# Reordering the tile loop of a routed expert layer on one core

## The chip, the core and the metric

The kernel runs on one core of a Trainium2 chip. The metric is the device time of one execution in microseconds (us). Engines are named as the profile names them: PE is TensorE (matmuls; PEld is its weight load), DVE is VectorE, ACT is ScalarE, POOL is GpSimd, SP is SyncE, which here only issues DMAs. Each engine works through its own queue in the order in which the kernel text issues its instructions.

## The reference

A long convolution by FFT, then two mixture-of-experts layers over the same 22784 tokens of width 128. Only the last layer is touched:

```python
logits = x @ w_gate + modality_bias[modality_id]
e_idx = np.argmax(logits, axis=1)
gate_w = softmax(logits)[arange(N), e_idx]
for e in range(E):                      # 8 experts, F = 1024
    mask = e_idx == e
    h = np.maximum(x[mask] @ w1[e], 0.0)
    out[mask] = gate_w[mask, None] * (h @ w2[e])
```

The token rows x of this layer are themselves a product: 32 softmax weights c per token times 32 slot outputs. The kernel folds those slot outputs into the first expert matrix, so a token's record is only its 32 weights, times its gate weight.

## The kernel before, in words

The first half of the span (convolution, first layer) is left as it is. Around 515 us the routing begins, and from about 538 us on the routed experts run in `routed_experts` (line 1175).

**Routing (class Routing, line 809).** Tokens are held as 178 groups of 128. The routing goes in parts (`CP`, line 39: groups 0 to 26, 26 to 64, 64 to 128, 128 to 178) and each part has chunks (`GB`, line 37). For a part: `choose` (argmax and softmax pieces), `offsets` (where each token's record goes; two matmuls, `pre`), and per chunk `prepare` (gate weight, position, masks); `table` (line 1032) makes the list that tells each tile of 256 tokens its place and its expert. These are some hundred small DVE instructions. `late_steps` (line 1155) hands them out one by one, each with a planned cost in us, and `spend(us)` (line 1371) issues as many as a credit allows; `need` (line 1376) issues all of them that a tile can't go on without, at once.

**Batches.** Two groups make a batch; there are 89. `prep(n)` (line 995) makes n batches (1 or 2): on DVE the product `m` (line 1006), on ACT its rounding into `hl` (line 1008, called the rounding here), on DVE the one-hot `oh` (line 1009) and two address columns (line 1011); its return value `rest` is the DVE subtraction (line 1015). `sort` (line 1019) then takes a batch: two matmuls (`srt`, line 1027), an ACT copy `so` (line 1029) and an indirect DMA on POOL that scatters the records to HBM (line 1144).

**Tiles.** There are 89 tiles. For tile k:

- `load_rec(k)` (line 1228): SP loads the records, two DMAs (lines 1234, 1235), after the scatters of all chunks up to the tile's own; `load_w(k)` (line 1242): SP loads the expert's weights into one of three buffers, skipped where the buffer holds them already, and only when the tile that used the buffer is done.
- `tokT(k)` (line 1249): two transposes on PE into `pst`, the addresses `ids` on DVE, and the cast `x` on ACT (line 1258).
- `l1(k, h)` for two halves (line 1260): 4 matmuls into `ph` (line 1267), ReLU on ACT into `hh` (line 1269), remainder on DVE into `hl` (line 1270).
- `l2(k, f)` for f = 0 to 7 (line 1272): 3 matmuls each into `acc` (lines 1280 to 1282).
- `out1(k)`: ACT copies `acc` to `yT` (line 1286); `out2(k)`: two transposes on PE into `pso`, ACT copy `y` (line 1293); `store`: two indirect DMAs on POOL (line 1305).

In PSUM, `pst`, `pso` and the table's `pr` share one buffer (tag t), `srt` and `pre` share another (tag s), and `ph` has two.

**The order in the loop (`run`, line 1310)** is written out by hand, and it is what sets the order on each engine. In loop step k it works on l2 of tile k, l1 of tile k+1, tokT of tile k+2, the records of tile k+3 and the output of tile k-1. On PE: l1(k+1) half 0, l2 f 0-1, pso(k-1), srt of the batch prepared in the step before, l2 f 2-3, l1(k+1) half 1, pst(k+2), l2 f 4-7. On ACT: yT, ReLU 0, y, so, rounding, ReLU 1, x. On DVE: remainder 0, routing, m and oh, remainder 1, ids, routing, subtraction, routing. `prep_to` (line 1198) says how many batches are prepared by step k: two per step up to step 6, then one per step, up to step 68. Ahead of the loop four batches are prepared and sorted, 5 us of routing (`PRE`) are issued, 16 matmuls on constants (`keep_warm`, line 1324) run on PE, and tile 0 and 1 are begun.

Of the kernel before, what the change touches and what calls it, by code (L numbers as in the profile page):

```python
# [15 lines left out]
I32 = mybir.dt.int32  # L16
# [7 lines left out]
NS, NE, F = 32, 8, 1024  # L24
# [4 lines left out]
NGR = NG // COLS  # L29
# [6 lines left out]
RW = 2 * NS + 2  # L36
GB = [0, 18, 22, 26, 34, 44, 54, 64, 80, 96, 112, 128, 144, 160, NG]
NC = len(GB) - 1
CP = (0, 3, 7, 11, NC)
PARTS = [(GB[a], GB[b], a, b) for a, b in zip(CP[:-1], CP[1:])]  # L40
PIECES = ((0, 7, 2), (7, 12, 3), (19, 16, 4), (35, 10, 3))
RT = NT // TM + 1
SPARE = NE * RT
PRE = 5.0
PACE = 0.25
GAP = 0.6
W1 = 4
W2 = 3
# [3 lines left out]
W6 = 3  # L52
W7 = 10
W8 = 4
W10 = 16
YBUF = 16
FAR = 1 << 20

# [750 lines left out]
class Routing:  # L809
# [185 lines left out]
    def prep(self, n):  # L995


        nc = self.nc
        i0 = self.prepped
        self.prepped += n  # L1000
        g0, n = COLS * i0, COLS * n
        g1 = g0 + n
        m = self.work("m", (4, BK, NS), 2)[:, :n]
        hl = self.rounded.tile([128, 4, BK, RW], F32R, name="hl4", tag="hl4", bufs=2)[:, :n]
        oh = self.rounded.tile([128, 4, LANES], F32R, name="oh", tag="oh", bufs=2)[:, :n]
        nc.vector.tensor_tensor(m, self.c[:, g0:g1].unsqueeze(2).to_broadcast([128, n, BK, NS]),  # L1006
                                self.gm[:, g0:g1].unsqueeze(3).to_broadcast([128, n, BK, NS]), op=ALU.mult)
        nc.scalar.copy(hl[:, :, :, :NS], m)
        nc.vector.tensor_tensor(oh, self.il.unsqueeze(1).to_broadcast([128, n, LANES]),
                                self.lane[:, g0:g1].unsqueeze(2).to_broadcast([128, n, LANES]), op=ALU.is_equal)  # L1010
        nc.vector.tensor_tensor(hl[:, :, :, 2 * NS:], self.eq[:, g0:g1].unsqueeze(3).to_broadcast([128, n, BK, 2]),
                                self.ab[:, g0:g1].unsqueeze(2).to_broadcast([128, n, BK, 2]), op=ALU.mult)

        def rest():
            nc.vector.tensor_tensor(hl[:, :, :, NS:2 * NS], m, hl[:, :, :, :NS].bitcast(F32), op=ALU.subtract)  # L1015
            self.batches += [(i0 + j, hl[:, COLS * j:COLS * j + COLS], oh[:, COLS * j:COLS * j + COLS]) for j in range(n // COLS)]
        return rest

    def sort(self, n, put):

# [154 lines left out]
def routed_experts(nc, tc, R, P, out, ro, tabs, put):  # L1175

    ident = P["ident"]
    with tc.tile_pool(name="p6", bufs=1, reuse_waits="tile") as sp, tc.tile_pool(name="p6p", bufs=1, space=PS, reuse_waits="tile") as pp:
# [8 lines left out]
        t, hid, x, acc, yT, ids = {0: new_rec()}, {0: new_hid()}, {0: new_x()}, {}, {}, {}  # L1187
# [6 lines left out]
        def due(k):  # L1194

            return GB[chunk_of(k) + 1] // COLS

        def prep_to(k):
            return min(NGR, max(due(k + 4), min(due(3) + 2 + 2 * k, 21 + k)))

        def prep(n):

            need(0, COLS * (ro.prepped + n))
            return ro.prep(n)

        def fill(e):

# [92 lines left out]
        def store(n, k1):  # L1300

            while n > 0 and outs and outs[0][0] <= k1:
                n -= 1
                k, j, d, y = outs.pop(0)
                i = nc.gpsimd.indirect_dma_start(out, bass.IndirectOffsetOnAxis(ap=d[:, j:j + 1], axis=0), y[:, j, :], None,  # L1305
                                                 bounds_check=NT - 1, oob_is_err=False)
                tc.declare_no_dep(i.ins, group="out", reason="every token is written once")
                tc.add_to_no_dep_group("out", i.ins)

        def run(k0, k1):  # L1310
            def go(f, k, *a):
                if k0 <= k < k1:
                    f(k, *a)
            go(load_rec, k0)
            go(load_w, k0, 2)
            while k0 == 0 and ro.prepped < due(3):
                prep(2)()
                ro.sort(2, put)
            for k in range(k0 + 1, k0 + 4):
                go(load_rec, k)  # L1320
                if k < k0 + 3:
                    go(load_w, k)
            spend(PRE)
            keep_warm(nc, pp, P["ones"], W10 if k0 == 0 else 0, tag="s", bufs=1)
            go(tokT, k0)
            for h in range(2):
                go(l1, k0, h)
            go(tokT, k0 + 1)
            for k in range(k0, k1):
                if 52 <= k < 52 + NE:  # L1330
                    fill(k - 52)
                go(out1, k - 1)
                if k > k0:
                    go(load_w, k + 2)
                    if not ro.batches:
                        go(load_rec, k + 3)
                go(l1, k + 1, 0)
                new = prep_to(k) - ro.prepped if k0 == 0 else 0
                assert new <= 2
                go(l2, k, 0, 1)  # L1340
                go(out2, k - 1)
                late_rec = k > k0 and len(ro.batches) > 0
                ro.sort(min(1, len(ro.batches)), put)
                spend(PACE)
                go(l2, k, 2, 3)
                ro.sort(len(ro.batches), put)
                if late_rec:
                    go(load_rec, k + 3)
                rest = prep(new) if new > 0 else None
                store(4, k - 2)  # L1350
                go(l1, k + 1, 1)
# [37 lines left out]
def build(nc, tc, I, O, dbg=None):  # L1389
# [13 lines left out]
    with tc.tile_pool(name="const", bufs=1) as cp:  # L1403
# [87 lines left out]
        close(prc)  # L1491
        close(plc)
        rqc, rq = pool("rq", side="right")
        tabs = [rq.tile([1, n, 3], I32, name=f"tab{i}") for i, n in enumerate((32, 32, 64))] + [rq.tile([1, 128 + 4, 3], I32, name="tab3")]
# [6 lines left out]
        with tc.manual_schedule():  # L1501
# [52 lines left out]
            ro.prep(1)()  # L1554
            run_all(seconds(0))
            ro.sort(1, put)
            ro.prep(2)()
            run_all(sums(0), seconds(1))
            push(1, 1)
            ro.sort(2, put)  # L1560
            adds.append(gate(3))
            for i in range(3):
                ro.prep(2)()
                if i == 1:
                    run_all(seconds(2, 3))
                ro.sort(2, put)
# [36 lines left out]
```

## Time and profile before

| what | us |
|---|---|
| median of 3 runs | 1064.74 (1056.84 to 1066.64) |
| the profiled execution | 1068.16 |
| its span, first to last instruction | 1066.3 |
| tiles 0 to 88, from the x of tile 0 to the last yT | 555.1 to 1056.0 |

Times below are from the start of the span. The tiles are told apart by the starts of their `yT` copies on ACT: tile k ends there.

### The profile page before, as it was taken

The numbers are of one execution on the slowest core, as the hardware profiler recorded it, in microseconds if no ns is written. First come the engines' busy times: TensorE is split into PE (matmuls) and PEld (weight loads), VectorE is DVE, ScalarE is ACT, GpSimd is POOL, SyncE is SP. The second block draws the span as 40 slices with busy tenths as digits, with TensorE's granted clock in tenths as the row PEclk, the third lists the DMA queues.
The fourth block names the chain that finished last, engine by engine and source line by source line (L and its number), as shares of the span: only waits on it lengthen the run. The fifth ranks groups of instructions, "written<-read, shape, count | busy, mean of one in ns | idle before, by whom it ended". The sixth has DMA issues, their size and how long they took to land.

```text
span 1066.3 us, 23059 instructions
## 1 busy us (share of the span) xinstructions
PE 929.7 (87%) x7758; PEld 834.5 (78%) x7758; DVE 709.8 (67%) x1445; ACT 594.8 (56%) x1141; POOL 515.2 (48%) x611
## 2 busy tenths in 40 slices
PE   6999999999997898999557777989888999898996
PEld 6888888888786897786246776888877888788996
DVE  1668677776775688953857767777776766564553
ACT  2565574755745556532324654666665666665673
POOL 2225737657388804531212644545554555555443
PEclk8999999999998999999668998999999999998998
DMA  9616748568478658999571221222222222222221
GB/s 279 173 38 178 243 147 252 164 200 244 132 242 290 239 141 309 360 406 340 157 237 27 61 53 46 64 56 64 64 59 56 64 69 77 61 64 56 61 63 40
DMA packets 135978, 156.66 MB, mean 147 GB/s; under 512 B 59823, under 2 KB 112975, under 8 KB 133436
## 3 DMA queue, kind: packets, MB, share of 16 engines
q1 hardware_dynamic: 125888, 137.43, 42.3%
q0 software_dynamic: 9968, 17.71, 5.1%
q8 instruction: 64, 1.05, 0.4%
q14 instruction: 58, 0.48, 0.1%
HBM read 227.39 MB, written 63.70 MB: 273 GB/s over the span
## 4 chain that ended last, share of the span: by engine, by line
PE 21%; DVE 9%; issue 8%; ACT 7%; POOL 2%; DMA 1%; another core or an unknown queue 1%; SPq 1%; POOLq 0%; ACTq 0%
PE ph L1267 6%; ACT hh L1269 6%; DVE hl L1270 5%; PE acc L1280 4%; PE acc L1281 4%; PE acc L1282 4%; PE srt L1027 2%; POOL out L1305 1%; PE pso L99 1%; DVE m L1006 1%; PE pst L99 1%; DVE hl L1015 1%; ACT x L1258 1%; DMA w<-s_w 1%
## 5 line engine op out<-in xcount | busy, mean ns | idle before, releaser
L1270 DVE SCALAR_TENSOR_TENSOR hl<-ph,hh 128x1024 fp32r<-128x1024 f32 x178 | 217.9, 1224 | 164.9 <-ACT hh L1269 116.9
L1305 POOL DMA_INDIRECT out<-y,ids x178 | 176.3, 990 | 89.5 <-issue 44.5
L1269 ACT ACTIVATE hh<-ph 128x1024 fp32r<-128x1024 f32 x178 | 182.1, 1024 | 63.4 <-PE ph L1267 38.2
L1280 PE MATMUL acc<-hh,w 128*128 128x256 f32 x712 | 211.6, 297 | 0.0
L1281 PE MATMUL acc<-hl,w 128*128 128x256 f32 x712 | 203.4, 286 | 0.0
L1282 PE MATMUL acc<-hh,w 128*128 128x256 f32 x712 | 203.3, 285 | 0.0
L1144 POOL DMA_INDIRECT s_rec<-so,dst x80 | 79.8, 997 | 179.7 <-ACT so L1029 158.1
L1267 PE MATMUL ph<-x,w 128*128 128x256 f32 x712 | 123.7, 297 | 45.8 <-ACT x L1258 30.7
L1267 PEld LDWEIGHTS ph<-x,w 128*128 128x128 f32 x712 | 99.2, 195 | 58.8 <-ACT x L1258 36.3
L1281 PEld LDWEIGHTS acc<-hl,w 128*128 128x128 f32 x712 | 138.0, 194 | 0.0
L1282 PEld LDWEIGHTS acc<-hh,w 128*128 128x128 f32 x712 | 138.0, 194 | 0.0
L1280 PEld LDWEIGHTS acc<-hh,w 128*128 128x128 f32 x712 | 137.4, 193 | 0.5 <-issue 0.4
L192 PEld LDWEIGHTS psx<-G,A 128*128 128x128 f32 x890 | 111.9, 196 | 19.8 <-DVE Y L203 13.2
L192 PE MATMUL psx<-G,A 128*128 128x128 f32 x890 | 124.5, 287 | 2.5 <-DVE A L137 1.3
L127 PE MATMUL psa<-fw,xs 128*128 128x180 f32 x640 | 109.8, 325 | 14.4 <-POOL xs L161 7.9
L127 PEld LDWEIGHTS psa<-fw,xs 128*128 128x128 f32 x640 | 99.6, 199 | 24.8 <-POOL xs L161 15.5
L137 DVE COPY A<-psa 64x360 f32<-64x360 f32 x160 | 88.4, 553 | 36.3 <-PE psa L127 32.0
L131 ACT COPY A<-psa 64x360 f32<-64x360 f32 x160 | 83.7, 523 | 41.1 <-PE psa L127 37.9
L216 ACT COPY yt<-psy 128x512 f32<-128x512 f32 (+1 forms) x92 | 52.7, 573 | 78.6 <-PE psy L99 54.0
L205 POOL TENSOR_TENSOR Y<-Y,V 128x256 f32<-128x256 f32 (+1 forms) x92 | 65.7, 714 | 62.9 <-DVE V L204 57.0
L203 DVE TENSOR_TENSOR Y<-psx,H 128x512 f32<-128x512 f32 (+1 forms) x92 | 61.9, 673 | 46.1 <-PE psx L192 45.4
L161 POOL COPY xs<-xr 89x512 f32<-89x512 f32 x68 | 45.7, 674 | 93.6 <-PE psa L127 73.7
(245 smaller groups left out, 1579.0 us busy)
## 6 DMA issues: line engine op xcount, KB each, us to landing
w<-s_w SPq DMA_DIRECT2D x88, 1536.0 KB
s_yt<-yt SPq DMA_DIRECT2D x88, 256.0 KB
xr<-x SPq DMA_DIRECT2D x16, 640.0 KB
xr<-s_yt SPq DMA_DIRECT2D x18, 512.0 KB
s_w<-ws SPq DMA_DIRECT2D x32, 256.0 KB
L<-s_yt SPq DMA_DIRECT2D x16, 512.0 KB
rt<-s_rec SPq DMA_DIRECT2D x89, 66.0 KB
rt<-s_rec SPq DMA_DIRECT2D x89, 64.0 KB
```

The lines of the kernel that those rows point to most:

```text
L127: nc.tensor.matmul(ps[:, i, :4 * NPAIR], x, fw1, start=True, stop=True)
L131: i = nc.scalar.copy(o, v)
L137: i = nc.vector.tensor_copy(o, v)
L192: nc.tensor.matmul(ps[:, m, :], A[:, 2 * i + m // 2, :, m % 2], G[:, 4 * i + m, :], start=True, stop=True)
L1144: d = nc.gpsimd.indirect_dma_start(rows, bass.IndirectOffsetOnAxis(ap=ro.dst[:LANES, i:i + 1], axis=0), o, None, bounds_check=SPARE * TB - ...
L1267: nc.tensor.matmul(ps[:, TM * j:TM * j + TM], w[k % 3][:, f:f + 128], x[k], start=True, stop=True)
L1269: nc.scalar.activation(o, ps, AF.Relu)
L1270: nc.vector.scalar_tensor_tensor(hl[:, 4 * h:4 * h + 4].rearrange("p j t -> p (j t)"), ps, 0.0, o.bitcast(F32), op0=ALU.max, op1=ALU.subtract)
L1280: nc.tensor.matmul(acc[k], wh, hh[:, f], start=(f == 0), stop=False)
L1281: nc.tensor.matmul(acc[k], wh, hl[:, f], start=False, stop=False)
L1282: nc.tensor.matmul(acc[k], wl, hh[:, f], start=False, stop=(f == 7))
L1305: i = nc.gpsimd.indirect_dma_start(out, bass.IndirectOffsetOnAxis(ap=d[:, j:j + 1], axis=0), y[:, j, :], None, bounds_check=NT - 1, oob_is ...
```

## The change

The loop's order is rewritten; no instruction of the tiles themselves changes. Per loop step k now:

- PE: l1(k+1) half 0, l2 f 0, pst(k+2), l2 f 1-2, pso(k-1), l2 f 3, l1(k+1) half 1, l2 f 4-5, srt, l2 f 6-7.
- ACT: yT, ReLU 0, x, y, ReLU 1, rounding, so.
- DVE: remainder 0, ids, subtraction of the batch prepared in the step before, m and oh of the new one, routing, remainder 1, routing twice.
- In steps 0 to 3 (`EARLY`) rounding, subtraction and sort of the two new batches stay in the same step, the rounding ahead of ReLU 1, the sorts ahead of l2 f 6-7.
- SP: weights of tile k+2 and records of tile k+3 at the head of each step. POOL: the two stores of tile k-2 split over the step, then the scatter.

Ahead of the loop, 7 routing steps come first, then two batches, tile 0's transposes and half 0, two more batches, tile 0's half 1, tile 1's transposes; the 16 constant matmuls are gone. Routing has five parts (0 to 26, 26 to 64, 64 to 96, 96 to 128, 128 to 178). The planned routing per step is 0.9 us, not 0.75. `pr` moves to the PSUM buffer of `srt`. Fewer batches are prepared in steps 4 to 18.

```diff
-CP = (0, 3, 7, 11, NC)
+CP = (0, 3, 7, 9, 11, NC)
-PACE = 0.25
+PACE = 0.9
+PACE2 = 0.9
+EARLY = 4
-W10 = 16
 def prep(self, n):
...
-        nc.scalar.copy(hl[:, :, :, :NS], m)
...
-        def rest():
+        def hi():
+            nc.scalar.copy(hl[:, :, :, :NS], m)
+
+        def lo():
             nc.vector.tensor_tensor(hl[:, :, :, NS:2 * NS], m, ...op=ALU.subtract)
...
-        return rest
+        return hi, lo
         def prep_to(k):
-            return min(NGR, max(due(k + 4), min(due(3) + 2 + 2 * k, 21 + k)))
+            smooth = due(3) + 2 + 2 * k if k < EARLY else k + 18 if k < 9 else min(27 + 13 * (k - 9) // 10, k + 21)
+            return min(NGR, max(due(k + 5) if k >= EARLY else 0, smooth))
 def run(k0, k1):
...
-            while k0 == 0 and ro.prepped < due(3):
-                prep(2)()
+            if k0 == 0:
+                run_late(7)
+                prep_all(2)
                 ro.sort(2, put)
-            for k in range(k0 + 1, k0 + 4):
+            for k in range(k0 + 1, k0 + 3):
                 go(load_rec, k)
-                if k < k0 + 3:
-                    go(load_w, k)
+                go(load_w, k)
+            go(tokT, k0)
+            go(l1, k0, 0)
+            if k0 == 0:
+                prep_all(2)
+                ro.sort(2, put)
+            go(l1, k0, 1)
+            go(load_rec, k0 + 3)
+            go(tokT, k0 + 1)
             spend(PRE)
-            keep_warm(nc, pp, P["ones"], W10 if k0 == 0 else 0, tag="s", bufs=1)
-            go(tokT, k0)
-            for h in range(2):
-                go(l1, k0, h)
-            go(tokT, k0 + 1)
+            new = None
             for k in range(k0, k1):
+                early = k0 == 0 and k < EARLY
+                old, new = new, None
...
                 if k > k0:
                     go(load_w, k + 2)
-                    if not ro.batches:
-                        go(load_rec, k + 3)
+                    go(load_rec, k + 3)
+                store(1, k - 2)
                 go(l1, k + 1, 0)
-                new = prep_to(k) - ro.prepped if k0 == 0 else 0
-                go(l2, k, 0, 1)
+                go(l2, k, 0)
+                go(tokT, k + 2)
+                go(l2, k, 1, 2)
+                if old:
+                    old[1]()
                 go(out2, k - 1)
-                late_rec = k > k0 and len(ro.batches) > 0
-                ro.sort(min(1, len(ro.batches)), put)
-                spend(PACE)
-                go(l2, k, 2, 3)
+                go(l2, k, 3)
+                n = prep_to(k) - ro.prepped if k0 == 0 else 0
+                if n > 0:
+                    new = prep(n)
+                    if early:
+                        new[0]()
+                spend(pace(k) / 3)
+                store(3 if k < k0 + 6 else 1, k - 2)
+                go(l1, k + 1, 1)
+                if new and not early:
+                    new[0]()
+                go(l2, k, 4, 5)
+                spend(pace(k) / 3)
+                if new and early:
+                    new[1]()
+                    new = None
                 ro.sort(len(ro.batches), put)
-                if late_rec:
-                    go(load_rec, k + 3)
-                rest = prep(new) if new > 0 else None
-                store(4, k - 2)
-                go(l1, k + 1, 1)
-                go(tokT, k + 2)
-                go(l2, k, 4, 5)
-                spend(PACE)
-                if rest:
-                    rest()
                 go(l2, k, 6, 7)
-                spend(PACE)
+                spend(pace(k) / 3)
...
-        ro.psum = lambda *a, **k: pp.tile(*a, tag="t", bufs=1, **k)
+        ro.psum = lambda *a, **k: pp.tile(*a, tag="s", bufs=1, **k)
```

`pace(k)` returns `PACE` or `PACE2`, both 0.9; `prep_all(n)` calls `prep(n)` and then both functions that it returns; `run_late(n)` issues n routing steps. In `build`, one more table (64 entries) is allotted for the fifth part, and `ro.prep(n)()` becomes `ro.prep_all(n)`.

## Rows read from the trace of the kernel before

**Rows 1.** Busy time by stretch: us, each engine's busy us (instructions), granted clock, DMA.

```profile
540.00:554.00 14.00, 8.91 (x37) 7.04 (x37) 7.27 (x22) 2.38 (x6) 3.74 (x4) 0.50 0.75 244
566.60:625.10 58.50, 45.99 (x322) 41.80 (x322) 40.99 (x108) 32.69 (x65) 29.39 (x29) 0.91 0.19 50
625.10:928.20 303.10, 263.45 (x2028) 245.51 (x2029) 214.57 (x520) 188.69 (x373) 156.98 (x160) 0.98 0.24 61
928.20:968.60 40.40, 37.88 (x306) 36.22 (x305) 27.26 (x54) 28.44 (x55) 23.11 (x23) 1.00 0.24 61
988.10:1052.90 64.80, 64.08 (x540) 63.58 (x539) 37.57 (x46) 44.01 (x74) 29.08 (x31) 1.00 0.24 59
```

**Rows 2.** Timeline of tiles 64 and 65: start us, us, engine, line, op [idle before].

```profile
944.18 1.03 ACT L1269 ACTIVATE hh<-ph 128x1024 fp32r<-128x1024 f32 x1 [0.62 <-ACT yT L1286]
...
945.24 1.22 DVE L1270 SCALAR_TENSOR_TENSOR hl<-ph,hh 128x1024 fp32r<-128x1024 f32 x1 [0.55 <-ACT hh L1269]
...
946.38 0.41 DVE L1006 TENSOR_TENSOR m<-c,gm 128x256 f32<-128x256 f32 x1
...
947.14 1.02 ACT L1269 ACTIVATE hh<-ph 128x1024 fp32r<-128x1024 f32 x1
...
948.06 0.36 ACT L1258 CAST x<-pst 128x256 fp32r<-128x256 f32 x1
...
948.48 0.74 PE L1267 MATMUL ph<-x,w 128*128 128x256 f32 x4 [0.34 <-ACT x L1258]
...
949.32 1.02 ACT L1269 ACTIVATE hh<-ph 128x1024 fp32r<-128x1024 f32 x1 [0.62 <-ACT yT L1286]
...
952.94 0.28 PE L1282 MATMUL acc<-hh,w 128*128 128x256 f32 x1
```

**Rows 3.** Timeline of tiles without a sort, 992 to 999 us.

```profile
992.12 0.66 PE L1267 MATMUL ph<-x,w 128*128 128x256 f32 x4
...
993.22 1.03 ACT L1269 ACTIVATE hh<-ph 128x1024 fp32r<-128x1024 f32 x1 [0.37 <-PE ph L1267]
...
996.36 0.66 PE L1267 MATMUL ph<-x,w 128*128 128x256 f32 x4
...
996.62 0.37 ACT L1286 COPY yT<-acc 128x256 f32<-128x256 f32 x1 [0.39 <-ACT x L1258]
...
996.86 0.28 PE L1280 MATMUL acc<-hh,w 128*128 128x256 f32 x1
...
997.06 1.03 ACT L1269 ACTIVATE hh<-ph 128x1024 fp32r<-128x1024 f32 x1
...
999.15 0.54 SPq L1235 DMA_DIRECT2D rt<-s_rec  x1
```

**Rows 4.** What PE waited for from 625 to 969 us: total, times, longest.

```profile
PE ph L1267 <- ACT x L1258: 19.8, 17, 6.3
...
PE pst L99 <- ACT y L1293: 3.5, 9, 0.7
```

**Rows 5.** Timeline of the start, 537 to 542 us; two batches prepared at a time.

```profile
537.65 0.69 DVE L1006 TENSOR_TENSOR m<-c,gm 128x512 f32<-128x512 f32 x1 [0.92 <-DMA s_rec<-A,dst]
...
539.03 0.69 DVE L1015 TENSOR_TENSOR hl<-m,hl 128x512 fp32r<-128x512 f32 x1 [0.22 <-ACT hl L1008]
...
539.77 0.71 PE L1027 MATMUL srt<-hl,oh 128*72 128x264 f32 x2 [1.37 <-DVE hl L1015]
...
541.07 0.71 PE L1027 MATMUL srt<-hl,oh 128*72 128x264 f32 x2 [0.58 <-ACT so L1029]
```

**Rows 6.** Timeline: single long waits at 654, 971 to 976 us.

```profile
653.89 1.22 PE L1267 MATMUL ph<-x,w 128*128 128x256 f32 x4 [6.30 <-ACT x L1258]
...
970.78 0.54 SPq L1235 DMA_DIRECT2D rt<-s_rec  x1
...
973.37 0.33 PE L99 MATMUL pst<-identr,rt 128*128 128x128 f32 x2 [2.14 <-DMA rt<-s_rec]
...
975.95 1.02 ACT L1269 ACTIVATE hh<-ph 128x1024 fp32r<-128x1024 f32 x1 [4.67 <-remote]
```

More of the change, by code (lines that the diff above doesn't have):

```diff
@@ L1012, in prep, with prep_all @@
                                 self.ab[:, g0:g1].unsqueeze(2).to_broadcast([128, n, BK, 2]), op=ALU.mult)
-        def rest():
+        def hi():
+            nc.scalar.copy(hl[:, :, :, :NS], m)
+        def lo():
             nc.vector.tensor_tensor(hl[:, :, :, NS:2 * NS], m, hl[:, :, :, :NS].bitcast(F32), op=ALU.subtract)
             self.batches += [(i0 + j, hl[:, COLS * j:COLS * j + COLS], oh[:, COLS * j:COLS * j + COLS]) for j in range(n // COLS)]
-        return rest
+        return hi, lo
+    def prep_all(self, n):
+        for f in self.prep(n):
+            f()
     def sort(self, n, put):
@@ L1204, in prep, with prep_all, run_late, pace @@
             return ro.prep(n)
+        def prep_all(n):
+            for f in prep(n):
+                f()
+        def run_late(n):
+            for _ in range(n):
+                next(late)
+        def pace(k):
+            return PACE if k < 10 else PACE2
         def fill(e):
@@ L1334, in run @@
                     go(load_w, k + 2)
-                    if not ro.batches:
-                        go(load_rec, k + 3)
+                    go(load_rec, k + 3)
+                store(1, k - 2)
                 go(l1, k + 1, 0)
-                new = prep_to(k) - ro.prepped if k0 == 0 else 0
-                assert new <= 2
-                go(l2, k, 0, 1)
-                go(out2, k - 1)
-                late_rec = k > k0 and len(ro.batches) > 0
-                ro.sort(min(1, len(ro.batches)), put)
-                spend(PACE)
-                go(l2, k, 2, 3)
-                ro.sort(len(ro.batches), put)
-                if late_rec:
-                    go(load_rec, k + 3)
-                rest = prep(new) if new > 0 else None
-                store(4, k - 2)
-                go(l1, k + 1, 1)
-                go(tokT, k + 2)
-                go(l2, k, 4, 5)
-                spend(PACE)
-                if rest:
-                    rest()
+                go(l2, k, 0)
[3 more added lines that the diff above has]
+                    old[1]()
+                go(out2, k - 1)
+                go(l2, k, 3)
+                n = prep_to(k) - ro.prepped if k0 == 0 else 0
+                assert n <= 2
+                if n > 0:
[12 more added lines that the diff above has]
+                    new = None
+                ro.sort(len(ro.batches), put)
                 go(l2, k, 6, 7)
-                spend(PACE)
+                spend(pace(k) / 3)
+            assert not new
             out1(k1 - 1)
@@ L1493, in build @@
         rqc, rq = pool("rq", side="right")
-        tabs = [rq.tile([1, n, 3], I32, name=f"tab{i}") for i, n in enumerate((32, 32, 64))] + [rq.tile([1, 128 + 4, 3], I32, name="tab3")]
+        tabs = [rq.tile([1, n, 3], I32, name=f"tab{i}") for i, n in enumerate((32, 32, 64, 64))] + [rq.tile([1, 128 + 4, 3], I32, name="tab4")]
         P["identr"] = rq.tile([128, 128], F32R, name="identr")
@@ L1553, in build @@
             run_all(offsets, ro.gates(*PARTS[0][:2]), ro.positions(*PARTS[0][:2]), ro.masks(*PARTS[0][:2]))
-            ro.prep(1)()
+            ro.prep_all(1)
             run_all(seconds(0))
             ro.sort(1, put)
-            ro.prep(2)()
+            ro.prep_all(2)
             run_all(sums(0), seconds(1))
@@ L1562, in build @@
             for i in range(3):
-                ro.prep(2)()
+                ro.prep_all(2)
                 if i == 1:
```

## The prediction

> **What bounds the kernel now.** I read the busy table by stretch first. Cut at the starts of the copies to yT, [rows 1] holds 8 tiles in its second stretch (tiles 1 to 8, 7.31 us each), 53 in the third (9 to 61, 5.72 each), 8 in the fourth (62 to 69, 5.05) and 15 in the last (73 to 87, 4.32). Only the last has no sorting. There PE is busy 64.08 of 64.80 us at full clock: PE is the bound. Before that it isn't: 263 of 303 us.
>
> Then the timeline, for what the sorting tiles wait on. Follow the ring in [rows 2]: ReLU 0 at 944.18, its remainder on DVE +1.06, m +1.14 (DVE works in order), then on ACT the rounding and ReLU 1, and x after them at 948.06, which is +1.68; PE may start the next l1 +0.42, and that gives the next ReLU 0 +0.84. Sum 5.14, the tile. PE needs less: from l1 at 948.48 to its last product at 952.94, plus one spacing of 0.12 (l1's four take 0.50, [rows 3]), is 4.58. The same tile without a sort is 996.36 - 992.12 = 4.24, so a batch's two sort matmuls cost PE 0.34. The view of waits agrees: l1 stood 17 times, 19.8 us, for x [rows 4]. Routing steps on DVE lengthen the ring, and where a batch can't go on without routing they come all at once: PE stood 6.30 us at 653.89 [rows 6].
>
> **The steady tile with one batch.** The new order takes the ring apart. x stands right behind ReLU 0; m comes a whole half ahead of remainder 1; rounding stands behind ReLU 1 and is used a tile later. What remains:
>
> - PE: 4.58, plus what the new order adds. pst and pso share one PSUM buffer, and pso(k-1) now comes soon after pst(k+2), so PE, in order, waits there for x to be read out, and all of l2 f 3 to 7 stands behind it. Count from l1's first matmul. ReLU 0 starts +0.70 (997.06 - 996.36 [rows 3]); x starts 0.92 later (948.06 - 947.14 [rows 2]); PE goes on 0.42 after that: 2.04. PE gets to pso at 0.50 for l1, 0.36 for f 0, about 0.2 for pst (two transposes, an estimate from the spacing), 0.72 for f 1-2: 1.78. Wait 0.26. Bounds: nothing, if ACT were earlier, to 0.68, if ReLU 0 starts +1.10 as at 993.22. I take 0.27. Tile 4.85.
> - DVE: 27.26 / 8 = 3.41 a tile with one batch and little routing [rows 1]. In the third stretch it is 214.57 / 53 = 4.05, so routing is 0.64 on the average tile; twice that still makes 4.7. Hidden, with little to spare.
> - ACT: 28.44 / 8 = 3.56. Hidden.
> - SP: records of tile k+3 are issued as late as before but needed earlier. Second record DMA 2.53 after yT (999.15 - 996.62 [rows 3]), usable 2.59 later (973.37 - 970.78 [rows 6]): 5.12 after yT. pst wants them one tile later, l1 + 0.86, that is 4.85 - 0.26 + 0.86 = 5.45 after yT. Hidden by 0.33 in a sorting tile; in the last tiles (4.51 a tile) by nothing, but a late pst only eats into the wait at pso.
> - POOL: 23.11 / 8 = 2.89 for two stores and a scatter. Hidden; but the scatter now stands behind the stores and late in the tile, which costs at chunk borders (below).
>
> At this place the Trainium skill has a word against the change. The row: with pst far from pso the shared buffer cost PE 3.5 us over 344 us [rows 4]. The page "Perfetto Trace Analysis" (Optimizing Tensor Performance, Matmuls) says that independent groups should go through different PSUM banks, so that one's copy-out lies beside the next one's matmuls; here the two are put next to each other on one. By the old row the cost would be under 0.1 us a tile and my forecast some 17 us lower; by the rule the copy-out shows, as counted above. I follow the count.
>
> **Tiles 9 to 69.** Before: 303.1 + 40.4 = 343.5 for 61 tiles. That is 61 x 5.14 = 313.5 for the ring and 30 above it: the burst at 653.89, the routing, and waits with no releaser such as the 4.67 "remote" at 975.95 [rows 6]. After: 61 x 4.85 = 296. The burst goes: in planned costs, part two is now 32 groups, some 6 us to its first masks, and from tile 4 to 12 eight us are spent, where before 64 groups wanted over 9 and 6.4 were spent. Add 4 for three tiles with two batches (a second sort waits for the first one's copy, 1.30 at half clock [rows 5]); add 4 for nine chunk borders, where the record load waits for a scatter that now comes late in the tile (about 0.45 each, an estimate: scatter out 0.8 later than the load's usual time, less 0.33); keep 12 of the waits without releaser, which no edit touches. 316. Gain 27.
>
> **Tiles 70 to 88.** No sort, so nothing to win, and the wait at pso comes in: 19 x 0.27 = 5 lost.
>
> **Tile 0 to 8.** 7 routing steps now stand ahead of the first batch on DVE: it moves from 537.65 to about 539.7. With 2.1 for preparing, two sorts at 1.30 and x's copy, tile 0's half 0 can start near 544 (an estimate), but DVE goes on to the second pair of batches only after remainder 0 (about 548), their sort stands on PE ahead of half 1, and 5 us of planned routing follow on DVE before tile 1's remainder 0 near 563. Then two more batches and their sort stand ahead of tile 0's f 6-7. I get 571 for its yT, against 566.6.
>
> In tiles 1 to 3 everything is one chain through DVE: l1 to ReLU 0 0.70, remainder +1.06, m +1.2, rounding and ReLU 1 +1.24, remainder 1 +1.06, routing and subtraction +1.5, sort +0.74 (539.77 - 539.03 [rows 5]), second sort +0.95 (of the 1.30), end of it and f 6-7 +1.04: 9.5. Three of them are 28.5, where the trace before has 23.2; with a forced table in tile 2 (nine steps, 0.5) 29. Tiles 4 to 8 have one batch: 5 x 4.85 = 24.3 where before 35.3, plus 3 for waits without releaser. Sum: +4.4 + 5.8 - 8 = +2: the early tiles lose what the next ones win. Removing the constant matmuls wins nothing: x of tile 0 stood behind them, but DVE sets the new start.
>
> **Sum.** +2 - 27 + 5 = -20 against the profiled execution: 1068.2 - 20 = 1048. That execution lies 3.4 us above the median; against the median 1064.7 the forecast is 1045.
>
> **Rivals.**
>
> 1. *Fewer waits without releaser.* If the 12 + 3 us kept above come from the tight ring and go with it, 1030. For: several coincide with PE standing for ACT. Against: they end with nothing that the profile names, and some lie in tiles without a sort. 0.15.
> 2. *Half clock in the early tiles.* In the start the granted clock is 0.50, that is 1.2 GHz [rows 1], though PE is busy 8.9 of 14 us, and in tiles 1 to 8 it is 0.91. The new early tiles leave PE idle nearly half of 9.5 us. At half clock the PE links of the chain (l1 0.5, two sorts 0.64, f 6-7 0.72, drain 0.3) double: 2.2 a tile, four tiles, 9 us: 1054 to 1055, within 1%. For: the constant matmuls that raised the clock are gone. Against: tiles 4 on are dense. 0.09. The page "TensorE: Matmul & The Clock Gate" (HAM oscillation — how this bites in real kernels) has this as its rule: bursts parted by waits fall back to half rate each time. By that rule the four tiles pay it; the trace before agrees in so far as l1 after the wait of 6.30 took 1.22, not 0.66 [rows 3, 6].
> 3. *Late records.* If record loads come 0.6 later under the earlier pst (scatters and stores in the same stretch of the tile), sorting tiles lose up to 0.6 - 0.33 beyond the wait at pso, the last ones 0.3 to 0.5: some 20 us, 1065, no change. For: 0.33 is little. Against: same queue, same place as before, and the one long wait for records was 2.14 in 89 tiles. 0.07.
> 4. *The routing doesn't spread.* The burst stays because credits run short: +8 and 2 more, 1055. Against: the count above. 0.04.
> 5. *Slower: the shared PSUM buffer.* If ReLU 0 starts +1.10 in the common tile, as at 993.22 [rows 3], the wait at pso is 0.68, not 0.27: +0.41 in 85 tiles, 35 us: 1080. It equals the kernel before from a wait of about 0.27 + 20 / 85 = 0.50. For: yT, ReLU 0 and x now stand in one row on ACT between acc's end and pso. Against: ReLU 0 at +0.70 in the undisturbed tile. 0.10.
>
> **How the numbers follow.** The forecast 0.55; its own range, from the spread of its estimates (early tiles 4, wait at pso 0.05 x 85), 1036 to 1054. Rivals 0.15, 0.09, 0.07, 0.04, 0.10. A measurement of this kernel tells about 1% from no change, that is 1054.1 and 1075.4. Faster: 0.55 + 0.15 = 0.70. Within: 0.09 + 0.07 + 0.04 = 0.20. Slower: 0.10. The range takes in rivals 1 to 4 (low end a little under the first) and leaves out the last: 1027 to 1066.
>
> **What would show it.** Right: in tiles 20 to 60 l1 no longer waits for x; pso waits for x about 0.27 in nearly every tile; tiles near 4.85 to 5.0; the last ones near 4.5, slower than 4.24; tiles 0 to 3 near 9.5 with the sort waiting for the subtraction on DVE; no burst near tile 12. Wrong: last tiles at 4.24 (buffer free in time), sorting tiles still over 5.1, pst waiting for records in most tiles, or an early stage that ends well before 625 us.

## The result, and the profile after

The changed kernel took 1074.36 us (median of 4 runs, 1071.71 to 1082.97) beside 1062.12 for the kernel before (4 runs, 1056.84 to 1066.64): a ratio of 1.0137 [1.0093, 1.0181], slower by 0.9 to 1.8%. The forecast was 1045. Later, on other chips, the same two kernels gave 1037.04 and 1041.78 (12 and 17 runs): 0.9950 [0.9934, 0.9967], faster by half a per cent, which is less than the 1% that the forecast took for no change. Both have to be explained.

Cut at the starts of the copies to `yT`, in us; e5 and e6 are the same two kernels again on one other chip, and e3 and e7 two variants (below). The last row counts TensorE's semaphore updates that came late (a semaphore update is the signal by which an engine tells the others that a result is ready); it is explained under the timeline.

| tiles | before | changed | e6: before | e5: changed | e3 | e7 |
|---|---|---|---|---|---|---|
| tile 0 ends at | 566.6 | 571.6 | 568.6 | 570.3 | 571.7 | 564.4 |
| 1 to 3 | 23.3 | 32.4 | 21.9 | 32.2 | 33.6 | 21.7 |
| 4 to 8 | 35.2 | 30.2 | 29.6 | 25.9 | 24.5 | 28.6 |
| 9 to 69 | 343.6 | 340.8 | 329.8 | 308.5 | 301.1 | 302.4 |
| 70 to 72 | 19.4 | 14.9 | 14.2 | 14.5 | 14.3 | 14.6 |
| 73 to 87 | 64.8 | 69.1 | 63.4 | 68.4 | 65.6 | 65.1 |
| after tile 87 | 13.4 | 13.3 | 13.4 | 13.3 | 13.3 | 13.4 |
| span | 1066.3 | 1072.4 | 1041.0 | 1033.1 | 1024.1 | 1010.1 |
| late updates, 9 to 69 | 107 of 370 | 160 of 374 | 0 of 370 | 0 of 374 | 2 of 374 | 2 of 374 |

The busy table by stretch of the changed kernel, for the stretches of [rows 1] and, first, for tiles 1 to 3 alone (us; busy us of PE, PEld, DVE, ACT, POOL; clock; DMA):

```profile
571.60:604.00 32.40, 21.33 (x126) 18.86 (x126) 16.63 (x52) 12.96 (x24) 9.05 (x10) 0.81 0.13 32
...
571.60:634.30 62.70, 47.59 (x326) 43.86 (x326) 36.49 (x100) 31.00 (x60) 23.14 (x24) 0.88 0.17 44
634.30:929.60 295.30, 254.67 (x2033) 239.64 (x2031) 221.86 (x553) 189.34 (x378) 166.30 (x162) 1.00 0.25 63
929.60:975.00 45.40, 39.01 (x314) 36.80 (x313) 25.82 (x49) 28.06 (x56) 27.71 (x27) 1.00 0.26 66
989.90:1059.10 69.20, 67.00 (x541) 63.81 (x540) 37.78 (x45) 45.70 (x75) 29.21 (x31) 1.00 0.23 56
```

From 634 to 930 us PE is busy 255 of 295 us at full clock. It still isn't the bound there, though the ring of [rows 2] is gone.

The timeline of the changed kernel (start, us, engine, line, operation [idle before, releaser]): the start, tile 1, a tile at 708 us, and two tiles without a sort.

```profile
539.22 0.69 DVE L1007 TENSOR_TENSOR m<-c,gm 128x512 f32<-128x512 f32 x1 [1.22 <-DMA s_rec<-A,dst]
...
577.07 1.22 DVE L1290 SCALAR_TENSOR_TENSOR hl<-ph,hh 128x1024 fp32r<-128x1024 f32 x1 [0.79 <-ACT hh L1289]
...
578.51 0.68 DVE L1018 TENSOR_TENSOR hl<-m,hl 128x512 fp32r<-128x512 f32 x1
...
579.34 0.44 PE L1034 MATMUL srt<-hl,oh 128*72 128x264 f32 x2 [3.35 <-DVE t_of L1095]
...
582.99 1.10 PE L1287 MATMUL ph<-x,w 128*128 128x256 f32 x4
...
708.08 0.64 PE L1287 MATMUL ph<-x,w 128*128 128x256 f32 x4
...
708.39 0.98 POOL L1325 DMA_INDIRECT out<-y,ids  x1 [0.30 <-issue]
...
709.27 0.41 PE L1034 MATMUL srt<-hl,oh 128*72 128x264 f32 x2
...
710.12 0.28 PE L1302 MATMUL acc<-hh,w 128*128 128x256 f32 x1
...
710.34 1.02 ACT L1289 ACTIVATE hh<-ph 128x1024 fp32r<-128x1024 f32 x1 [1.93 <-PE srt L1034]
...
1008.22 0.37 ACT L1306 COPY yT<-acc 128x256 f32<-128x256 f32 x1 [0.47 <-PE acc L1302]
...
1009.99 0.20 PEld L100 LDWEIGHTS pso<-ident,yT 128*128 128x128 f32 x2 [0.25 <-ACT x L1278]
...
1012.85 0.37 ACT L1306 COPY yT<-acc 128x256 f32<-128x256 f32 x1 [0.53 <-PE acc L1302]
```

Where the forecast held: the start (539.22 for the first m, 539.7 forecast; [rows 5] had 537.65), tile 0 (571.6; 571), the wait of pso for x in the tiles without a sort (4.57 in the common tile, 4.63 in the one shown, beside 4.24 in [rows 3]), no burst near tile 12, and in tile 1 a sort that stood 3.35 us for remainder, routing steps and subtraction on VectorE.

Where it failed is the tile at 708 us. The second half of l1 starts at 708.08 and its four matmuls follow within 0.4. ReLU 1 needs nothing else, yet starts only at 710.34, when TensorE has already finished the tile; the view names the sort, for which ReLU 1 doesn't wait. The trace also records the semaphore events, which the views don't list: the update of that l1 was due at 708.73 and arrived at 710.32, those of the sort and of acc at 710.41 and 710.49, all three almost together. Meanwhile a store ran on GpSimd. I call an update late if it arrives more than 0.2 us behind its usual delay (0.30 after the start of a group's last matmul, 0.24 for pst; 0.01 after an instruction's end on ScalarE and VectorE; an update without a record of its own is dated by the next record, so its time is an upper bound, and counts are good to a few). In tiles 9 to 69 the kernel before has 107 such of TensorE, the changed one 160.

The waits of the changed kernel in tiles 9 to 69 (engine, line, waited for: us in total, times, longest):

```profile
ACT hh L1289 <- issue: 18.6, 30, 4.2
ACT hh L1289 <- PE srt L1034: 17.8, 11, 2.0
ACT hh L1289 <- PE ph L1287: 12.5, 15, 1.3
...
ACT so L1036 <- PE acc L1302: 11.5, 24, 0.7
...
PE pso L100 <- ACT x L1278: 24.7, 47, 1.8
...
PE srt L1034 <- ACT so L1036: 4.4, 4, 1.6
```

ReLU "waits" 11 times for a sort and 30 times for nothing, and the copy `so` 24 times for acc: each a wait whose true releaser signalled late. Counted by the true releaser, ReLU stood 49.5 us behind late updates of l1 in these tiles, in 57 waits; in the kernel before 18.0 us, in 27. l1's wait for x of [rows 4] is gone.

### The profile page after: what moved, and what is told of

Read it like the earlier page. It is cut to its first block, busy times and chain, and to the rows that moved or that the text cites. A ratio compares the mean times of both kernels' runs of the same rounds, so it can differ in the third digit from the quotient of the medians.

```text
span 1072.4 us, 22977 instructions
## 1 busy us (share of the span) xinstructions
PE 924.5 (86%) x7732; PEld 830.5 (77%) x7732; DVE 715.5 (67%) x1481; ACT 596.0 (56%) x1141; POOL 520.7 (49%) x613
## 3 DMA queue, kind: packets, MB, share of 16 engines
q8 instruction: 64, 1.05, 0.4%
## 5 line engine op out<-in xcount | busy, mean ns | idle before, releaser
L1325 POOL DMA_INDIRECT out<-y,ids x178 | 184.5, 1036 | 98.0 <-issue 46.2
L1300 PE MATMUL acc<-hh,w 128*128 128x256 f32 x712 | 217.8, 306 | 0.0
L1302 PE MATMUL acc<-hh,w 128*128 128x256 f32 x712 | 203.7, 286 | 0.0
L1151 POOL DMA_INDIRECT s_rec<-so,dst x80 | 76.7, 959 | 171.2 <-ACT yT L1306 86.2
L1287 PE MATMUL ph<-x,w 128*128 128x256 f32 x712 | 118.4, 290 | 5.0 <-DMA w<-s_w 5.0
L128 PE MATMUL psa<-fw,xs 128*128 128x180 f32 x640 | 110.9, 327 | 13.4 <-POOL xs L162 7.1
```

What stands on the lines that cost most here:

```text
L128: nc.tensor.matmul(ps[:, i, :4 * NPAIR], x, fw1, start=True, stop=True)
L1151: d = nc.gpsimd.indirect_dma_start(rows, bass.IndirectOffsetOnAxis(ap=ro.dst[:LANES, i:i + 1], axis=0), o, None, bounds_check=SPARE * TB - ...
L1287: nc.tensor.matmul(ps[:, TM * j:TM * j + TM], w[k % 3][:, f:f + 128], x[k], start=True, stop=True)
L1300: nc.tensor.matmul(acc[k], wh, hh[:, f], start=(f == 0), stop=False)
L1302: nc.tensor.matmul(acc[k], wl, hh[:, f], start=False, stop=(f == 7))
```

## The experiments

**e1 to e4: without the stores, and two edits of the changed kernel.** The edit of e1 (changed kernel) and e2 (kernel before):

```diff
-            for j in range(2):
+            for j in range(0 if 10 <= k < 67 else 2):
                 outs.append((k, j, d, y))
```

> The changed kernel, with the output stores of tiles 10 to 66 left out (GpSimd issues no indirect store there; the scatters stay). Theory 1, held signals: in the trace of the changed kernel the semaphore updates of TensorE that fall due 1.0 to 1.8 us after the start of a store on GpSimd arrive only at about 1.85, with the first packets of that store; the new order puts the second half of l1 and the sort there, so that ReLU 1 starts 1.0 to 1.6 late in some 18 of 61 tiles and the copy to so 0.6 late in most. Without stores those waits go: tiles 9 to 69 fall from 340.8 to about 318, one-batch tiles from 5.10 to about 4.85, the whole to about 1050. Theory 2, the new order's own chain (ReLU 0, x, pso, y, ReLU 1, so, yT in one row on ScalarE) makes 5.1: GpSimd is not in it, tiles 9 to 69 stay at 336 to 341, the whole at 1068 to 1074.

> The kernel before, with the output stores of tiles 10 to 66 left out. Theory 1: there the held signals fall mostly on pso and the sort, whose copies are not in the ring ReLU 0, remainder 0, m, rounding, ReLU 1, x, l1 of 5.14; ReLU 1 is late in 5 cases only. So little is won: tiles 9 to 69 from 343.6 to about 335, the whole near 1054. If it wins as much as the changed kernel does (over 18 us), the stores cost both orders alike and do not explain why the change failed.

e3 and e4:

```diff
-            ps = pp.tile([128, 2, 128], F32, name="pst", tag="t", bufs=1)
+            ps = pp.tile([128, 2, 128], F32, name="pst", tag="s", bufs=1)
```
```diff
                 go(out2, k - 1)
-                go(l2, k, 3)
...
                 go(l1, k + 1, 1)
+                go(l2, k, 3)
```

> The changed kernel with pst in the PSUM buffer of the sort instead of the one it shares with pso; nothing else. The wait of pso for x (30.7 us in 55 waits in the changed kernel's trace) goes. In the tiles without a sort, where nothing else is late, a tile falls from 4.57 to 4.24: 16 tiles, 5 us. Theory 1 (held signals set the sorting tiles): there little more comes, the whole falls by 5 to 10 us. Theory 2 (the shared buffer is what the forecast underrated): sorting tiles fall by 0.25 to 0.3 too, the whole by about 20 us.

> The changed kernel with the second half of l1 one product group earlier (ahead of l2 f 3 instead of behind it), 0.36 us sooner on TensorE. Theory 1: the stores start when so has been scattered, so the stretch in which signals are held does not move, and half 1 now mostly signals before it: the 18 late ReLU 1 become fewer than 6, tiles 9 to 69 fall by 10 to 18 us. Theory 2 (the chain on ScalarE): ReLU 1 still waits for y and starts hardly earlier: 0 to 5 us.

All four ran on a chip where the kernel before took 1042.43 (22 runs). e1: 1036.65, 0.9931 [0.9905, 0.9957]. e2: 1040.58, 0.9986 [0.9966, 1.0007]. e3: 1025.55, 0.9825 [0.9792, 0.9858]. e4: 1037.78, 0.9952 [0.9933, 0.9971]. e1 falls even below theory 1's number (309.6 for tiles 9 to 69, where it said 318), but e4, with all stores, has 309.1 too: in none of the four traces do more than 5 of TensorE's updates come late in these tiles, with stores or without. So theory 1 was not tested here, and on this chip the stores cost neither order much. What was tested: the shared buffer (theory 2 of e3: the sorting tiles fall too, though the whole by 11.5 us beside e5 below, not 20), and in e4 the place of the second half of l1, which gains nothing beside e5's 1037.04 below. e3's one-batch tiles take 4.56, e1's and e4's 4.86.

**e5 to e7: the two kernels again, and a version with the old start.** e7 is e3 with the prologue and, for tiles 0 to 3, the tile body of the kernel before:

```diff
-            if k0 == 0:
-                run_late(7)
+            while k0 == 0 and ro.prepped < due(3):
                 prep_all(2)
                 ro.sort(2, put)
...
             for k in range(k0, k1):
...
+                if k0 == 0 and k < EARLY:
...
+                    continue
                 store(1, k - 2)
```

> The changed kernel itself, beside the kernel before. In the first pair of traces TensorE's semaphore updates came late after stores (31 of 88 for ph and 43 of 62 for the sort in tiles 9 to 69); in the traces of the four variants not one did, with or without stores, and there the kernel before took 1042 us and not 1062. Theory 1: the late updates belong to the chip or its moment, not to the order of the kernel. Then where they are absent the changed kernel has one-batch tiles of 4.86, about 312 us for tiles 9 to 69 and 1037 to 1040 us in all, 0.2 to 0.6% below the kernel before; and where they are present again it is 1070 to 1080 and 1% above. Theory 2: the changed order itself (pst beside pso) brings them about, and the variants were cured by their edits: then 1054 to 1058 us beside 1042, and late updates in the trace.

> The kernel before itself, for a trace from the same chip as the changed kernel's. Theory 1: no late updates of TensorE; the ring of 5.14 stays, since it doesn't hang on them; the burst of routing near tile 12 stays (two tiles of 11.2 and 7.6); tiles 9 to 69 take about 331 us instead of 343.6 and the tiles without a sort 4.24. Theory 2 (the late updates are part of this kernel): about 343 us for these tiles.

> The changed kernel with pst in the sort's PSUM buffer, and with the beginning of the kernel before: its prologue (all first batches sorted ahead of tile 0, constant matmuls, no early routing) and its tile body for tiles 0 to 3; the new order from tile 4 on. Theory 1 (in tiles 0 to 3 the new order puts preparing, sorting and remainders in one chain through VectorE inside the tile, 9.5 to 12 us a tile, where the old body spreads it over two tiles): tile 3's yT comes 15 to 16 us earlier than with the new start (at 589 instead of 605), tiles 4 to 8 stay near 25, and the whole falls by about 14, to 1010 to 1013 where the kernel before takes 1042. Theory 2 (the early tiles wait for the routing itself, whatever the order): what tiles 0 to 3 win comes back as waits in tiles 4 to 13, and the whole falls by less than 5.

On a third chip: e5 1037.04 beside 1041.78, 0.9950 [0.9934, 0.9967]; e6 1042.84 (one run); e7 1013.04, 0.9728 [0.9701, 0.9754]. Hardly any late updates in all three. Theory 1 held for all three: the late updates are not the order's own, and with the old start tile 3 ends at 586.1 instead of e3's 605.3, of which tiles 4 to 69 give back 5.5. The waits of e5 in tiles 9 to 69, and a tile of its timeline:

```profile
ACT y L1313 <- PE pso L100: 33.2, 61, 0.6
ACT hh L1289 <- PE ph L1287: 30.0, 61, 1.2
...
PE pso L100 <- ACT x L1278: 7.3, 42, 0.2
PE pst L100 <- DMA rt<-s_rec: 5.5, 9, 1.6
```
```profile
916.37 0.64 PE L1287 MATMUL ph<-x,w 128*128 128x256 f32 x4
...
917.11 1.03 ACT L1289 ACTIVATE hh<-ph 128x1024 fp32r<-128x1024 f32 x1
...
918.03 0.36 ACT L1278 CAST x<-pst 128x256 fp32r<-128x256 f32 x1
...
918.45 0.44 PE L100 MATMUL pso<-ident,yT 128*128 128x128 f32 x2 [0.17 <-ACT x L1278]
...
919.75 1.02 ACT L1289 ACTIVATE hh<-ph 128x1024 fp32r<-128x1024 f32 x1 [0.46 <-PE ph L1287]
...
921.22 0.64 PE L1287 MATMUL ph<-x,w 128*128 128x256 f32 x4
```

This is the tile as forecast: from l1 to l1 4.85, ReLU 0 at +0.74 (0.70), x 0.92 later (0.92), pso 2.08 after l1 (2.04). ReLU 1 is released by ph, the operation it waits for, 0.67 after l1's first matmul (919.08); at 708 us it took 2.26. In e3's timeline the transposes to pso no longer wait for x, which is copied beside them:

```profile
907.10 0.37 ACT L1306 COPY yT<-acc 128x256 f32<-128x256 f32 x1 [0.24 <-PE acc L1302]
...
908.50 0.36 ACT L1278 CAST x<-pst 128x256 fp32r<-128x256 f32 x1
908.59 0.38 PE L100 MATMUL pso<-ident,yT 128*128 128x128 f32 x2
...
911.66 0.37 ACT L1306 COPY yT<-acc 128x256 f32<-128x256 f32 x1 [0.22 <-PE acc L1302]
```

So the shared buffer costs 4.86 - 4.56 = 0.30 in a common tile. Tiles 9 to 69 as a whole fall by 7.4 us only, from 308.5 to 301.1: l1 to l1 is shorter, but the waits of pst for records grow from 5.5 to 9.1. The forecast had counted 0.27 against the old row's 0.1. The rule of the Trainium skill, "Perfetto Trace Analysis", Optimizing Tensor Performance / Matmuls, by which groups should rotate through PSUM banks, agrees with this trace.

**e8, e9 and e12: x alone.** From the kernel before; e9 and e12 are one kernel, with the routing in five parts (and one more table for the fifth) besides:

```diff
-                go(l1, k + 1, 1)
                 go(tokT, k + 2)
+                go(l1, k + 1, 1)
```
```diff
-CP = (0, 3, 7, 11, NC)
+CP = (0, 3, 7, 9, 11, NC)
-PACE = 0.25
+PACE = 0.3
```

> The kernel before with one line moved: the transposes to pst and the copy to x stand ahead of the second half of l1 instead of behind it. Nothing else of the change. Theory 1: of all that the change moves, x alone opens the ring of 5.14: without ReLU 1 in it the ring is 1.06 + 1.14 + 0.4 + 0.4 + 0.42 + 0.84 = 4.3, under TensorE's 4.58, and pso, far from pst here, doesn't wait. Where no updates come late, one-batch tiles fall from 5.13 to about 4.6, tiles 9 to 69 from 330 to about 304, the whole from 1042 to about 1016. Theory 2: m, the rounding and the subtraction on their old places close the ring again through ReLU 1 and remainder 1, so that the change needed all its moves: tiles stay over 5.0 and the whole above 1035.

> The same, and the routing in five parts as in the change, with 0.30 us paid per call in place of 0.25. Theory 1: the burst at tiles 12 and 13 (11.2 and 6.8 us in the kernel before, 7.6 above two common tiles) is the larger part two, and goes with it: 6 to 8 us less than with x alone, about 1009. Theory 2: the routing costs VectorE the same in whatever parts, and comes back spread over other tiles: under 2 us.

> The kernel before with x ahead of the second half of l1 and the routing in five parts, once more. On a chip with late updates 0.9995 of the kernel before again: pso's updates are late in 56 of 61 tiles there and the sort's copy and the one to yT behind it wait. On a chip without: theory 1 (x alone opens the ring) 4.6 a one-batch tile, tiles 9 to 69 near 300, the whole 1008 to 1012 beside 1042; theory 2 (rounding and subtraction close it again): above 1030.

e8 and e9 fell on a chip where the kernel before took 1063.65: 1064.92, 1.0014 [0.9986, 1.0042], and 1062.72, 0.9995 [0.9968, 1.0022]. Late updates are back in both (154 and 135 of 370 of TensorE's in tiles 9 to 69), so they decide nothing on the ring. e12, on a chip where the kernel before took 1040.55, has none to speak of and took 1039.16, 0.9989 [0.9973, 1.0006]: theory 2 for the whole. l1 no longer waits for x, but in the stretch with routing (640 to 840 us) the next ring shows, first in the waits, then in the timeline:

```profile
PE srt L1027 <- DVE hl L1015: 26.7, 30, 1.3
```
```profile
674.76 1.23 DVE L1270 SCALAR_TENSOR_TENSOR hl<-ph,hh 128x1024 fp32r<-128x1024 f32 x1 [1.27 <-ACT hh L1269]
...
675.90 0.41 DVE L887 SCALAR_TENSOR_TENSOR xr<-xr,small 128x256 f32<-128x256 f32 x1
...
676.23 0.42 DVE L1015 TENSOR_TENSOR hl<-m,hl 128x256 fp32r<-128x256 f32 x1
...
676.71 0.47 PE L1027 MATMUL srt<-hl,oh 128*72 128x264 f32 x2 [0.93 <-DVE hl L1015]
```

Remainder 1, a routing step, the subtraction, and the sort right behind it: TensorE stood 30 times for the subtraction. The change puts the sort a tile behind the subtraction; in e5 all waits of the sort in tiles 9 to 69 come to 3 us. Five parts do take the burst away (tiles 12 and 13 take 5.70 and 5.44; in e6 11.20 and 6.76), but tiles 14 to 50 rise from 5.36 to 5.54 on average and eat it (they also pay 0.9 us of routing instead of 0.75). Where the routing is done theory 1 holds in part: tiles 51 to 68 take 4.88 on average, in e6 5.13, so there x alone does open the ring. The edit of e8 by itself never met a chip without late updates.

**e10, e11 and e13 to e15: what holds the updates.** e10 repeats e1, e11 and e15 repeat e7, on whichever chip came. e13 and e14 are e7 with part of the stores left out:

```diff
-            for j in range(2):
+            for j in range(0 if 20 <= k < 39 else 2):
```

> The changed kernel with the output stores of tiles 10 to 66 left out, once more, for a chip with late updates (four chips so far: two where in the trace semaphore updates of all engines come late within 2 us of the start of an indirect DMA on GpSimd and never later, and the kernel before takes 1062 to 1064; two where none comes late and it takes 1042). Theory 1, the stores hold them: on a chip with late updates, tiles 9 to 69 take 310 to 318 us here as on the other chips (309.6), since one launch a tile is left (the scatter) in place of three, and late updates fall from some 90 to under 30 in this stretch. Theory 2, such a chip holds updates whatever GpSimd does, and the stores only stand beside them: 330 us or more and as many late updates. On a chip without late updates: 1036 again.

> The changed kernel with pst in the sort's buffer and the old start, once more. On a chip without late updates 1013 again, beside 1042. On one with late updates, theory 1 (the new order has no slack behind ph, the sort and acc, where the held updates fall; the spare PSUM buffer takes only the wait for x off) gives tiles 9 to 69 at 330 to 338 and 1045 to 1052 beside 1063; theory 2 (the shared buffer was what made held updates costly, since x's late copy stopped TensorE): about 320 and 1033.

> The variant with pst in the sort's PSUM buffer and the old start, with the output stores of tiles 20 to 38 left out, so that tiles 23 to 40 run without stores and tiles 42 to 61 with them, in one execution. Without late updates tiles 23 to 40 take 82 us with or without stores, tiles 42 to 61 96 us. On a chip with late updates: theory 1 (the launches of stores hold them) gives under 10 late updates and 82 to 85 us in tiles 23 to 40, and over 30 late ones and 101 to 106 us in tiles 42 to 61; theory 2 (the chip holds them whatever GpSimd does) gives late updates at the same rate in both and 88 us or more in the first. On a chip without late updates: 82 and 96, about 1013, and the question stays open.

> The same kernel as in the run before (stores of tiles 20 to 38 left out), for a chip with late updates; the same two theories and numbers: tiles 23 to 40 without stores 82 to 85 us and under 10 late updates if the launches hold them, 88 us or more and as many late ones as with stores if the chip does it by itself. Without late updates 82 and 96 us again.

> The variant with pst in the sort's buffer and the old start, complete. On a chip with late updates: from the run before, tiles with stores take 5.45 to 6.1 us there against 5.04 elsewhere, so tiles 9 to 69 come to 340 or so and the whole to 1066 to 1070 beside a kernel before at 1063 to 1069: nothing left. If the rival holds, that the loss stands only in part of the tiles, 1045 to 1055. On a chip without late updates 1013 to 1017 beside 1042.

e10, e11 and e13 fell on chips without late updates: 0.9929 [0.9902, 0.9957], 0.9760 [0.9735, 0.9785] and 0.9823 [0.9774, 0.9873] (e13's end, behind its last store, took 7 us longer than e7's, and so did e14's; why stays open). e14 fell on one with them: 1060.43 beside 1068.79, 0.9920 [0.9886, 0.9954]. Tiles 24 to 40 (no stores) and 43 to 61 (with stores) in the table by stretch of e14 (columns as in [rows 1]):

```profile
712.60:794.20 81.60, 78.95 (x654) 76.71 (x654) 72.46 (x190) 62.38 (x121) 15.85 (x18) 1.00 0.19 43
805.30:908.80 103.50, 93.41 (x727) 87.56 (x726) 71.14 (x165) 67.08 (x134) 58.62 (x57) 0.98 0.25 67
```

and of e13, the same kernel on a chip without late updates:

```profile
701.60:783.40 81.80, 79.04 (x655) 76.80 (x654) 72.55 (x190) 62.43 (x121) 15.88 (x18) 1.00 0.20 43
792.50:888.00 95.50, 90.10 (x729) 87.20 (x728) 72.09 (x166) 69.31 (x133) 55.34 (x57) 0.98 0.28 72
```

Without stores the two chips agree, 81.6 and 81.8; with them the one with late updates needs 8 us more for 19 tiles. Late updates of TensorE: 12 of 104 in e14's first stretch (more than the "under 10" of theory 1; a scatter a tile is left), 43 of 115 in its second. The two stretches of one execution hold different tiles; the same tiles 24 to 40 with their stores are in e15, on e14's chip, and in e7, on a chip without late updates:

```profile
713.95:805.35 91.40, 82.44 (x653) 77.08 (x652) 73.49 (x192) 61.00 (x121) 52.02 (x51) 1.00 0.24 63
691.60:773.30 81.70, 78.99 (x654) 76.76 (x653) 72.62 (x190) 62.45 (x120) 50.18 (x51) 1.00 0.27 71
```

So on the chip with late updates the stores cost these 17 tiles 91.4 - 81.6 = 9.8 us (35 of 104 updates of TensorE late, not 12), and on the other nothing. This is the stores' doing; whether their launches or the data that they move hold the updates, no run separates. e15 as a whole took 1066.90 beside 1067.52 on that chip, 0.9985 [0.9956, 1.0015], as expected from e14: nothing of e7's 2.7% is left there. Its tiles 9 to 69 took 348.0 (340 or so expected), beside 302.4 in e7: a buffer of its own for pst doesn't cure the late updates, which is against e11's theory 2, and the loss is larger than its theory 1 had it.

## Why the prediction was wrong

**The step that failed** is in "Tiles 9 to 69": "keep 12 of the waits without releaser, which no edit touches". Those waits were late updates: the "remote" wait of 4.67 [rows 6] is one, an update of l1 due at 971.25 and recorded at 975.93, behind a row of store launches. They are not a constant. With late updates and without, tiles 9 to 69 take 343.6 and 329.8 in the old order, 13.8 us more; 340.8 and 308.5 in the new one, 32.3 more, where the forecast kept 12. What they cost depends on which operation's update falls behind a store, and that is what the order sets. Of TensorE's late ones in tiles 9 to 69, the kernel before has 33 of ph, 32 of pso, 21 of the sort, 15 of acc; the changed kernel 62, 14, 41 and 27. In the old ring a late pso delays y, which stands ahead of a rounding that waits for m anyway (kernel before, 625 to 969 us):

```profile
ACT hl L1008 <- DVE m L1006: 42.1, 39, 7.1
```

In the new order a late ph delays ReLU 1 and all of f 4 to 7 behind it, as in the tile at 708 us; a late sort delays so, which stands right ahead of yT on ScalarE. That ReLU's waits carry most of it is read from the 49.5 and 18.0 us above; no run separates the four operations, and in e15, with some 33 late ones of ph, 48 of the sort and 38 of acc, the shares are others. Measured: 340.8, forecast 316. On the chips without late updates the same tiles took 308.5, and the same sum without those 12 us is 304.

The other terms, forecast, first pair, and e6 to e5:

| term | forecast | first pair | e6 to e5 |
|---|---|---|---|
| tile 0 | +4.4 | +5.0 | +1.7 |
| tiles 1 to 3 | +5.8 | +9.2 | +10.3 |
| tiles 4 to 8 | -8 | -5.0 | -3.8 |
| tiles 9 to 69 | -27 | -2.8 | -21.3 |
| tiles 70 to 87 | +5 | -0.2 | +5.2 |
| sum (span) | -20 | +6.1 | -7.9 |

- One-batch tile: 4.85 forecast, 4.85 to 4.86 measured in e5. PE-bound part: 4.58 forecast, 4.56 in e3. Mechanism and size right.
- Tiles 9 to 69, e6 to e5: 6 us less won than forecast. 4.5 of them are 308.5 beside the 304 above; the rest is that without late updates the kernel before loses 13.7 (329.8, not 343.5) and the forecast only its 12. Records cost 5.5 us in nine waits (4 forecast).
- Tiles 1 to 3: the chain through VectorE is there, but a tile takes 10.6, 12.1 and 9.8 (e5: 10.9, 11.4, 9.9), not 9.5. l1 after each wait took 1.05 to 1.10 instead of 0.64, where the granted clock is 0.50; from 571.6 to 604.0 it is 0.81 on the mean: rival 2, which the forecast held at 0.09, came true in part, for these three tiles. The page it named (the Trainium skill, "TensorE: Matmul & The Clock Gate", HAM oscillation) is right on the direction. The tiles lie about 1 us above the forecast each, half of what that rival gave; only the 0.4 of l1 in it is seen to be the clock's.
- Tiles 73 to 87: +0.27 forecast, 4.57 - 4.24 = +0.33 measured. Right. In the first pair tiles 70 to 72 won 4.5 back, but only because the stall of 4.67 [rows 6] came one tile earlier, on the other side of the cut (below); tiles 69 to 72 together won 1.5, and tiles 9 to 68 5.8 instead of 2.8.

```profile
974.08 1.03 ACT L1289 ACTIVATE hh<-ph 128x1024 fp32r<-128x1024 f32 x1 [4.24 <-issue]
```

- The rivals: "fewer waits without releaser" had the right object and the wrong sign. The shared buffer as a slower case was priced at 0.68; its wait grew to 24.7 / 47 = 0.53 in the first pair, where updates come late, and is 7.3 / 42 = 0.17 without them.

So even where nothing comes late the gain is 0.5%, not 1.9%: some 12 of the 21 us won go to tiles 0 to 3. That is shown by e7, which takes them back and, with pst out of the shared buffer, is the version that beats both kernels: 0.9728 and 0.9760 on two chips, and 0.9985 of the kernel before on one with late updates.

## What to carry to other kernels

A wait that ends with no releaser, or with one the instruction doesn't wait for, is a fact to be explained before it is kept as a constant: look up when the true releaser's semaphore event arrived, and what ran just ahead of it. When an order is tightened, ask which signals now have no slack, not only which engine is free. And measure a change of a per cent on more than one chip: here the same edit is 1.4% slower on one and 0.5% faster on another.

## What the runs showed of the hardware

On some chips semaphore updates of TensorE, ScalarE and VectorE are held behind a launch of an indirect DMA on GpSimd. (As far as recorded, each chip but one was met at one time only, so a chip's property and its state at the moment can't be told apart; the one met twice, by e14 and e15, held updates both times.) By the time between the start of the last such launch and the moment an update was due, from 545 to 1040 us, updates of TensorE, ScalarE and VectorE together (late, all):

| due after the launch, us | six executions with late updates | eleven without |
|---|---|---|
| 0 to 0.4 | 562 of 1998 | 15 of 4237 |
| 0.4 to 0.8 | 507 of 2028 | 14 of 3280 |
| 0.8 to 1.2 | 1100 of 2191 | 10 of 3412 |
| 1.2 to 1.6 | 647 of 974 | 0 of 2150 |
| 1.6 to 2.0 | 109 of 604 | 0 of 1370 |
| over 2.0 | 3 of 2880 | 0 of 5583 |

A store holds GpSimd 0.98 us, its first packets run about 1.55 after its start, and held updates of TensorE arrive at a median of 1.84 (first four executions), when the packets are on their way. (The first rows also hold updates still held by the launch before, 1.27 earlier; a row of launches held one of l1 for 4.7.) Records are missing too in these executions: VectorE has 1014 for 1260 updates in the changed kernel, 1261 in e5, and an update without one counts by the next. TensorE has 1086 of 1160, and its rows alone say the same: 250 of 294 late at 1.2 to 1.6, 3 of 648 over 2.0. The Trainium skill, "Perfetto Trace Analysis", DMA Instruction — SWDGE (GPSIMD), says that the profile ends such an instruction when its descriptors are written, not when the data moves; 0.98 and 1.55 agree. That updates wait meanwhile, no run explains: what on such a chip differs stays open. The packets' delay after a launch is the same on both kinds of chip. The kernel before took 1062 to 1069 on the chips with late updates (the first pair's, that of e8 and e9, that of e14 and e15) and 1041 to 1042 on four others.
